# Sliding-window attention into a gated feed-forward: tile 0's values from v as loaded, and 24 unread matrix products ahead of the first turn

## The chip, the cores and the metric

The kernel runs on one core of one Trainium2 chip. The metric is the device time of one execution in microseconds, lower being better. One profiled execution of the kernel gives the trace that is read here. Engines are named as in the profile: PE is TensorE (PEld its weight loads), DVE VectorE, ACT ScalarE, POOL GpSimd, SP SyncE, which only issues transfers.

## The reference

Eight batches of eight heads, 576 positions, head dimension 64. A position sees itself and the 63 before it. The attention output, 4608 rows of 512, goes through h·cos(h) between two matrices.

```python
scores = (1 / sqrt(64)) * q @ k.T                      # q, k, v: (8, 8, 576, 64) f32
rel = pos[:, None] - pos[None, :]
scores = where((rel >= 0) & (rel < 64), scores, -1e9)
attn = exp(scores - max(scores)); attn = attn / sum(attn)
x = (attn @ v).transpose(0, 2, 1, 3).reshape(4608, 512)
h = x @ w_in                                           # (512, 2048)
out = (h * cos(h)) @ w_out                             # (2048, 512) -> (4608, 512) f32
```

## The kernel before

**Tiles and groups.** The 4608 rows are cut into nine tiles of 512 rows (`mt` 0 to 8). A row block has 64 positions, so a batch has nine blocks (`j` 0 to 8), and tile 0 is blocks 0 to 7 of batch 0. Heads go in four pairs (`p`). A block attends to itself and to the block before it: 128 columns of scores for each of the 64 rows of two heads, which makes a unit of 128 x 128. Four units are a group; tile 0 has eight, two for each pair (`g` 0 and 1).

**The steps of a group**, each one or a few instructions: scores on PE (`s`), the row maximum negated on DVE (`m`), four exponentials with their sums on ACT (`e`), the reciprocal of the sums on DVE (`i`), the product of both on POOL or DVE (`n`, tile `w`), four transposes on PE into `tw_ps` (`w`) and a copy to `wT` on DVE or ACT (`c`). When both groups of a pair are there, PE multiplies them with v (`v`, tile `o_ps`) and an engine copies the result to the pair's quarter of `xT` (`x`). Before all that, PE transposes q and k of the pair (`tq`, `tk`) and an engine copies them (`pq`, `pk`). A suffix d, a or p names DVE, ACT or POOL.

**v and its shifted copies.** Block j needs the values of blocks j-1 and j on 128 partitions. The transfers of `load_v` bring blocks 0 and 1 to slot 0 of the tile `v`, 2 and 3 to slot 2, and so on to slot 6, and block 8 to half of slot 7. An odd block finds its two halves in one slot. For an even one the step `z` (`spread_v`) copies halves into the odd slots: block 2 beside block 1 in slot 1, and so on. For batch 0 POOL copies four upper halves (`z.1.p`) and DVE three lower ones (`z.0.d`).

**The feed-forward.** For each of sixteen slices of 128 columns (`ff`) PE adds four products of 128x512, one per pair (`ks`), in `h_ps`; ACT takes the sine, DVE multiplies (`gT`), and PE multiplies by `w_out`. Of tile 0's 64 products some run ahead, as soon as a pair's `xT` is there: `h.0` and `h.1` (three slices each of pairs 0 and 1), `hx.3`, `hx.4` (two products each), and `hl` (pairs 2 and 3 of five slices). The rest follows without a gap in the list.

**What sets the order.** All engines take their instructions strictly in the order in which the program issues them. For tile 0 that order is the string `FIRST`, a list of step names with pair, group and engine; `l` issues the next transfer of a list (`w_in` in three parts, q and k of batch 1, `w_out` in two parts). For all later work, times are given to functions and a loop (`pump`) issues them between the feed-forward's products. In PSUM five named banks and three tiles with the tag "t" are shared by all of these; `H_FIRST` names the banks of `h_ps` in tile 0, `S_FIRST` those of its scores.

Of the kernel before, what the change touches and what calls it, by code (L numbers as in the profile page):

```python
# [10 lines left out]
def _safe_warn(msg, *a, **kw):  # L11
# [3 lines left out]
F32 = mybir.dt.float32  # L15
BF16 = mybir.dt.bfloat16
AF = mybir.ActivationFunctionType
ALU = mybir.AluOpType
# [7 lines left out]
GF = 4  # L26
# [5 lines left out]
PAIRS = 4  # L32
# [3 lines left out]
SKEW = 3  # L36
# [2 lines left out]


FIRST = (
# [6 lines left out]
)  # L48


# [1 line left out]
def kernel(  # L52
# [9 lines left out]
    nc = tc.nc  # L62
    B, H, S, D = q.shape
# [5 lines left out]
    MT = 512  # L69
    TU = MT // 64  # L70
# [4 lines left out]
    att = ctx.enter_context(tc.tile_pool(name="att", bufs=3))  # L75
# [10 lines left out]
    ident = const.tile([128, 128], BF16, name="ident")  # L86
# [5 lines left out]
    st = {}  # L92

    H_FIRST = ("O1", "X0", "X1", "S", "O0") * 3 + ("X0",)
    H_SECOND = ("X0", "X1", "S", "O0", "O1") * 3 + ("t",)
    H_BANKS = ("X0", "O0", "X1", "S", "O1") * 2 + ("X0", "X1", "S", "O0", "O1", "t")
    S_BANKS = ("X1", "S", "X0")
# [3 lines left out]
    def bank(which, name):  # L103
        if which == "t":
            return ps_t.tile([128, 512], F32, tag="t", name=name)
        return ps.tile([128, 512], F32, tag=which, name=name)

    def copy(engine, out, in_):
        {"a": nc.scalar.copy, "p": nc.gpsimd.tensor_copy}.get(engine, nc.vector.tensor_copy)(out, in_)  # L109
# [18 lines left out]
    def halves(tile_):  # L128
        return {name: tile_[:, i * PAIRS * S:i * PAIRS * S + PAIRS * S].rearrange("p (a x) -> p a x", a=PAIRS)
                for i, name in enumerate(("q", "k"))}  # L130

    def rows(b):
        return rowtiles[1 if b == 1 else 0]
# [22 lines left out]
    def values_of(b):  # L156
        return rowtiles[0][:, 0:8 * d_model].rearrange("p (s x) -> p s x", s=8) if b == B - 1 else vtiles[b % 3]

    def load_v(b, c):
        n = 128 if c < 4 else 64  # L160
        vt = values_of(b)[:n, 2 * c if c < 4 else 2 * c - 1]
        nc.gpsimd.dma_start(out=vt.rearrange("p (h d) -> p h d", h=H),  # L162
                            in_=v[b, :, c * 128:c * 128 + n, :].rearrange("h p d -> p h d"))


    def spread_v(b, half, engine="p"):
        vt = values_of(b)
        to, of = ((vt[0:64, 1:7:2], vt[0:64, 2:8:2]), (vt[64:128, 1:8:2], vt[64:128, 0:7:2]))[half]
        if engine == "dma":
            nc.sync.dma_start(out=to, in_=of)  # L170
        else:
            copy(engine, to, of)

    def load_w_in(lo, hi):
        nc.gpsimd.dma_start(out=w_in_sb[:, :, lo:hi], in_=w_in_v[:, :, lo:hi])
# [15 lines left out]
    def put(name, b, p, engine=None):  # L191
        of = st.pop(("t" + name, b, p)).rearrange("d (c p) -> d p c", c=RC)
        to = halves(turned(b))[name][:, p].rearrange("d (p c) -> d p c", c=RC)
        if b or name == "k":
            copy(engine, to, of)
        elif engine == "a":
            nc.scalar.mul(to, of, scale)
        else:
            nc.vector.tensor_scalar(to, of, scale, None, ALU.mult)
# [98 lines left out]
    def g_norm(n, engine="p"):  # L298
        (e, _), rden = st.pop(("e", n)), st.pop(("r", n))
        w = att.tile([128, GF, 128], BF16, tag="w", name="w", bufs=8)  # L300
        u = len(groups[n])
        (nc.gpsimd if engine == "p" else nc.vector).tensor_tensor(out=w[:, 0:u], in0=e[:, 0:u], op=ALU.mult,  # L302
                                in1=rden[:, 0:u].unsqueeze(2).to_broadcast([128, u, 128]))
        st["w", n] = w

    def g_trans(n):
        w, u = st.pop(("w", n)), len(groups[n])
        if n in direct:
            st["tw", n] = t_ps = ps_t.tile([128, GF, 128], BF16, tag="t", name="tw_ps")
            for i in range(u):  # L310
                nc.tensor.transpose(t_ps[:, i], w[:, i], ident)  # L311
            return
        wT = att.tile([128, GF, 128], BF16, tag="wT", name="wT", bufs=20)
        nc.sync.dma_start(out=wT[:, 0:u], in_=w[:, 0:u].rearrange("p u c -> p (u c)"), transpose=True)
        st.update({("wT", unit): wT[:, i] for i, unit in enumerate(groups[n])})

    def g_put(n, engine=None):
        wT, u = att.tile([128, GF, 128], BF16, tag="wT", name="wT", bufs=20), len(groups[n])
        copy(engine, wT[:, 0:u], st.pop(("tw", n))[:, 0:u])
        st.update({("wT", unit): wT[:, i] for i, unit in enumerate(groups[n])})  # L320


    def values(mt, p):
        st["o", mt, p] = o_ps = bank("S", "o_ps") if mt > 1 and p == PAIRS - 1 else ps_t.tile([128, MT], F32, tag="t", name="o_ps")
        for i in range(TU):
            b, j = divmod(mt * TU + i, NU)
            wT = st["wT", (b, p, j)]
            cross = st["cross", (b, p, j)]
            for h in range(2):
                nc.tensor.matmul(out=o_ps[64 * h:64 * h + 64, 64 * i:64 * i + 64],  # L330
                                 lhsT=values_of(b)[:, max(j - 1, 0), 128 * p + 64 * h:128 * p + 64 * h + 64],
                                 rhs=wT[:, 64 * (h ^ cross):64 * (h ^ cross) + 64], start=True, stop=True, skip_group_check=True)


    def put_x(mt, p, engine=None):
        if ("xT", mt) not in st:
            st["xT", mt] = att.tile([128, PAIRS, MT], BF16, tag="xT", name="xT", bufs=2)
        o_ps = st.pop(("o", mt, p))
        copy(engine, st["xT", mt][:, p], o_ps)
# [8 lines left out]
    def first(mt, ff, ks, start, stop):  # L348
        if start:
            st["h", ff] = bank((H_FIRST, H_SECOND, H_BANKS)[min(mt, 2)][ff], "h_ps")  # L350
        nc.tensor.matmul(out=st["h", ff], lhsT=w_in_sb[:, ks, ff * 128:ff * 128 + 128],  # L351
                         rhs=st["xT", mt][:, ks], start=start, stop=stop)

    def skew(mt):
        return 5 if mt < 2 else SKEW

    def last_pairs(mt):
        for ff in range(skew(mt)):
            for ks in range(2, PAIRS):
                first(mt, ff, ks, False, ks == PAIRS - 1)  # L360

    def skewed(mt, ks, n):
        for ff in range(skew(mt) if mt else SKEW):
            first(mt, ff, ks, n == 0, n == PAIRS - 1)

    def last_rows(gT, o_sb):
# [27 lines left out]
    n = n_first  # L394
# [67 lines left out]
    def cast(name, engine):  # L462
        copy(engine, halves(rows(0))[name][:, 0], first_f32[name])
# [10 lines left out]
    def load():  # L474
# [3 lines left out]
    turn_s, turn_h = iter(range(100)), iter(range(100))  # L478
    steps = {"tq": lambda p: transposed("q", 0, (p,)), "tk": lambda p: transposed("k", 0, (p,)),
             "pq": lambda p, engine=None: put("q", 0, p, engine),  # L480
             "pk": lambda p, engine="a": put("k", 0, p, engine),
             "mk": put_masks, "ck": lambda: cast("k", "d"), "l": load, "tb": sine_table, "h": lambda p: skewed(0, p, next(turn_h)), "hl": lambda: last_pairs(0),
             "hx": lambda ff: [first(0, ff, ks, ks == 0, False) for ks in range(2)],
             "z": lambda half, engine=None: spread_v(0, half, engine),
             "s": lambda p, g: g_scores(2 * p + g, next(turn_s) % 5), "m": lambda p, g: g_max(2 * p + g),
             "e": lambda p, g: g_exp(2 * p + g), "i": lambda p, g: g_inv(2 * p + g),
             "n": lambda p, g, engine: g_norm(2 * p + g, engine), "w": lambda p, g: g_trans(2 * p + g),
             "c": lambda p, g, engine=None: g_put(2 * p + g, engine), "v": lambda p: values(0, p),
             "x": lambda p, engine=None: put_x(0, p, engine)}
    for step in FIRST.split():  # L490
        name, *args = step.split(".")
        steps[name](*[int(a) if a.isdigit() else a for a in args])
    load_v(0, 4)
    for c in range(5):
        load_v(1, c)

    for mt in range(n_mt):
# [11 lines left out]
        for ff in range(n_ff):  # L509
# [8 lines left out]
            e = ff % 2  # L518
# [58 lines left out]
```

## Time and profile before

| | us |
|---|---|
| median of 3 runs | 306.96 |
| lowest and highest run | 306.51, 307.69 |
| the profiled execution | 306.41 |
| its span, first to last instruction | 304.4 |
| PE busy in the span | 288.7 (95%) |
| ACT busy | 235.7 (77%) |
| DVE busy | 220.4 (72%) |
| POOL busy | 171.1 (56%) |

All times in the views count from the span's start; 2.0 us of the profiled execution lie around the span. In a row of the timeline stand the start, the duration, the engine, the line, the operation, the tile written and the tile read with their shapes, and how many instructions are merged; in brackets stands idle time just before, with what ended it. Matmuls overlap, so that the start of the next one tells more than the end.

### The profile page before, as it was taken

What the parts mean: (1) busy time and instruction counts of PE and PEld (TensorE: products, weight loads), DVE (VectorE), ACT (ScalarE), POOL (GpSimd) and SP (SyncE); (2) the same over time, 40 slices, a digit from 0 to 9 for tenths busy, and PEclk for the clock granted to TensorE, in tenths of its full rate; (3) what the DMA queues carried; (4) which work ended last, traced back from release to release, by engine and by line L of the source; (5) the groups of instructions that cost most, each with busy time, mean ns of one, the idle gap of its engine ahead of it and who ended that gap; (6) DMA issues with size and microseconds to landing.
All of it is one profiled execution on the core that took longest, in us unless ns stands there. A gap on an engine that the chain in (4) does not pass through costs nothing.

```text
span 304.4 us, 7847 instructions
## 1 busy us (share of the span) xinstructions
PE 288.7 (95%) x2628; PEld 142.1 (47%) x2668; DVE 220.4 (72%) x834; ACT 235.7 (77%) x786; POOL 171.1 (56%) x198
## 2 busy tenths in 40 slices
PE   3769999999999999999999999999999999999996
PEld 3544444544454445444544444444444454454443
DVE  3896889588787878787877787778778877236701
ACT  5997799967997799779987998799869986106600
POOL 8996257977774976497659665967433630000000
PEclk9989999999999999999999999999999999999999
DMA  7999999699969999999999979999994441011012
GB/s 150 181 211 207 207 155 139 105 165 191 225 114 155 225 164 132 154 201 183 138 167 208 189 106 172 157 219 123 180 172 110 87 130 62 0 72 70 0 69 71
DMA packets 165577, 43.88 MB, mean 144 GB/s; under 512 B 154720, under 2 KB 160800, under 8 KB 165536
## 3 DMA queue, kind: packets, MB, share of 16 engines
q0 software_dynamic: 99344, 18.06, 75.1%
q1 hardware_dynamic: 66048, 25.11, 40.2%
q8 instruction: 21, 0.34, 0.5%
q14 instruction: 20, 0.16, 0.2%
q10 hardware_dynamic: 144, 0.20, 0.2%
HBM read 36.70 MB, written 9.44 MB: 152 GB/s over the span
## 4 chain that ended last, share of the span: by engine, by line
PE 88%; DVE 6%; issue 2%; ACT 2%; DMA 1%; POOL 0%; DVEq 0%; POOLq 0%
PE h_ps L351 41%; PE out_ps L534 36%; PE o_ps L330 3%; PE s_ps L261 3%; DVE negm L273 1%; PE out_ps L371 1%; DMA first_f<-in_q_dram 1%; DVE w L302 1%; PE tq_ps L186 1%; DVE s L277 1%; DVE v L109 1%; PE tk_ps L186 1%; PE tw_ps L311 1%; PE s_ps L244 1%; ACT e L288 1%
## 5 line engine op out<-in xcount | busy, mean ns | idle before, releaser
L351 PE MATMUL h_ps<-xT,w_in 128*128 128x512 bf16 x556 | 127.1, 381 | 2.2 <-DVE xT L109 0.6
L534 PE MATMUL out_ps<-w_out,gT 128*128 128x512 bf16 x543 | 123.0, 379 | 1.8 <-issue 1.1
L522 DVE TENSOR_TENSOR gT<-h_ps,sin 128x512 bf16<-128x512 f32 x144 | 95.4, 688 | 33.6 <-ACT sin L519 33.4
L519 ACT ACTIVATE sin<-h_ps 128x512 f32<-128x512 f32 x144 | 82.9, 599 | 34.1 <-PE h_ps L351 32.8
L288 ACT ACTIVATE e<-s,negm 128x128 f32<-128x128 f32 x256 | 98.6, 388 | 0.3 <-DVE negm L277 0.3
L302 POOL TENSOR_TENSOR w<-e,rden 128x512 bf16<-128x512 f32 (+1 forms) x76 | 74.5, 993 | 31.5 <-DVE rden L295 29.1
L351 PEld LDWEIGHTS <-w_in 128*128 128x128 bf16 x576 | 56.0, 98 | 67.1 <-issue 2.7
L534 PEld LDWEIGHTS <-gT 128*128 128x128 bf16 x560 | 53.2, 98 | 62.4 <-issue 0.2
L277 DVE CUSTOM_DVE_ANT_0 s<-s_ps,mask 128x128 f32<-128x128 f32 x256 | 58.0, 284 | 0.1
L288 ACT ACTIVATION_READ_ACCUMULATOR e<-s,negm 128x1 f32 x256 | 48.1, 188 | 0.0
L149 POOL DMA_DIRECT2D rows<-in_q_dram x30 | 25.4, 867 | 25.9 <-DMA T<-rows 16.6
L162 POOL DMA_DIRECT2D v<-in_v_dram x35 | 29.8, 879 | 10.5 <-DMA rows<-in_k_dram 7.3
L109 ACT COPY out_sb<-out_ps 128x512 f32<-128x512 f32 (+1 forms) x18 | 10.1, 563 | 24.2 <-PE out_ps L534 18.7
L295 DVE RECIPROCAL rden<-den 128x4 f32<-128x4 f32 (+1 forms) x80 | 13.8, 172 | 19.2 <-ACT e L288 18.6
L149 POOL DMA_DIRECT2D rows<-in_k_dram x30 | 25.5, 897 | 2.2 <-DMA T<-rows 2.2
L109 DVE CAST xT<-o_ps 128x512 bf16<-128x512 f32 x27 | 17.6, 679 | 6.5 <-PE o_ps L330 6.3
L277 DVE DVE_READ_ACCUMULATOR2_ANT negm<- 128x1 f32 x256 | 21.2, 83 | 0.0
L109 DVE COPY out_sb<-out_ps 128x512 f32<-128x512 f32 x18 | 12.4, 689 | 12.0 <-PE out_ps L534 12.0
L288 ACT ACTIVATE e<-s_ps,negm 128x128 f32<-128x128 f32 x32 | 11.5, 425 | 1.6 <-DVE negm L273 1.6
L261 PE MATMUL s_ps<-T 64*64 64x128 bf16 x512 | 12.1, 221 | 0.0
L261 PEld LDWEIGHTS <-T 64*64 64x64 bf16 x512 | 8.2, 106 | 8.3 <-DVE negm L277 4.4
L330 PEld LDWEIGHTS <-v 128*64 128x64 bf16 x504 | 9.5, 112 | 4.3 <-issue 2.1
(56 smaller groups left out, 146.2 us busy)
## 6 DMA issues: line engine op xcount, KB each, us to landing
out_dram<-out_sb SPq DMA_DIRECT2D x16, 512.0 KB, 6.1
v<-in_v_dram POOLq DMA_DIRECT2D x28, 128.0 KB, 8.3
rows<-in_q_dram POOLq DMA_DIRECT2D x24, 128.0 KB, 5.2
rows<-in_k_dram POOLq DMA_DIRECT2D x24, 128.0 KB, 7.8
w_out<-in_moe_w_out_dram POOLq DMA_DIRECT2D x2, 1024.0 KB, 16.7
w_in<-in_moe_w_in_dram POOLq DMA_DIRECT2D x2, 768.0 KB, 12.4
wT<-w SPq DMA_TRANSPOSE x66, 3.9
out_dram<-out_sb SPq DMA_DIRECT2D x3, 256.0 KB, 2.0
```

The source lines that it names most:

```text
L109: {"a": nc.scalar.copy, "p": nc.gpsimd.tensor_copy}.get(engine, nc.vector.tensor_copy)(out, in_)
L149: nc.gpsimd.dma_start(out=rows(b)[lo:lo + n, slot * 512:slot * 512 + 512].rearrange("p (h d) -> p h d", h=H), in_={"q": q, "k": k}[name][b ...
L162: nc.gpsimd.dma_start(out=vt.rearrange("p (h d) -> p h d", h=H), in_=v[b, :, c * 128:c * 128 + n, :].rearrange("h p d -> p h d"))
L261: nc.tensor.matmul(out=s_ps[cross][to, u].rearrange("p (a t) -> p a t", a=2), lhsT=q_cols(b, p, j)[d], rhs=k_cols(b, p, j)[d], start=True, ...
L277: nc.vector.tensor_tensor_reduce(out=s[:, u], in0=s_ps[:, u], in1=mask[:, 2 - j % 2 if j else 0], scale=-scale if b else -1.0, scalar=BIG, ...
L288: nc.scalar.activation(e[:, u], s[:, u], AF.Exp, bias=negm[:, u:u + 1], scale=1.0 if n < n_first else -1.0, accum_out=den[:, u:u + 1])
L302: (nc.gpsimd if engine == "p" else nc.vector).tensor_tensor(out=w[:, 0:u], in0=e[:, 0:u], op=ALU.mult, in1=rden[:, 0:u].unsqueeze(2).to_br ...
L330: nc.tensor.matmul(out=o_ps[64 * h:64 * h + 64, 64 * i:64 * i + 64], lhsT=values_of(b)[:, max(j - 1, 0), 128 * p + 64 * h:128 * p + 64 * h ...
L351: nc.tensor.matmul(out=st["h", ff], lhsT=w_in_sb[:, ks, ff * 128:ff * 128 + 128], rhs=st["xT", mt][:, ks], start=start, stop=stop)
L519: nc.scalar.activation(sin, h_ps, AF.Sin, bias=math.pi / 2.0)
L522: nc.vector.tensor_tensor(out=gt[:, e], in0=h_ps, in1=sin, op=ALU.mult)
L534: nc.tensor.matmul(out=o_ps[e], lhsT=gT[ff // 2][:, ff % 2, ms * 128:ms * 128 + 128], rhs=w_out_sb[:, ff], start=ff == 0, stop=ff == n_ff - 1)
```

## The change

Tile 0 no longer uses the odd slots of v. `values_first` takes v as it was loaded. An odd block is one product over 128 partitions, as before. An even block is a product over its own 64 rows (the lower half of its slot) and another over the 64 rows of the block before it (the upper half of the slot before). Step `va` issues the first two kinds, step `vb` the products over the block before (`over` in the code). The last pair's are all in `va.3`; there those of the third kind go to a bank of their own (`o2`), and the step `xl` adds them: ACT copies `o2` to SBUF, DVE casts the odd blocks and adds the even ones. Both spreading copies go; block 8, which tile 1 uses, keeps one copy (`spread_last`, on POOL, after tile 0).

The step `warm.24` puts 24 products of the 128 x 128 identity with itself ahead of the first transpose; nothing reads their result.

The list is written in another order. The product of group (1, 0) goes from DVE to POOL, that of group (3, 1) is halved between DVE and POOL (`nh`); `pk.3` and `c.1.0` go from ACT to DVE; `c.3.0` and `x.1` go from DVE to ACT; the transfers of k of batch 1 and of `w_out` are issued behind the last product on POOL. Ahead of `hl` there are now two slices of pairs 0 and 1 and one pair of products (`hx.2`), six products where there were ten; `hl` has three slices instead of five.

On DVE, from the reciprocal of the first group of pair 1 on (`rden` the reciprocals, `negm` the maxima, `w` the product, `v` the spreading copy), before:

```order
L295 RECIPROCAL rden_383<-den_366 128x4
L273 TENSOR_REDUCE negm_385<-s_ps_313 128x4
L302 TENSOR_TENSOR w_396<-e_365,rden_383 128x512
L295 RECIPROCAL rden_404<-den_377 128x4
L273 TENSOR_REDUCE negm_406<-s_ps_348 128x4
L109 COPY wT_434<-tw_ps_324 128x512
L109 COPY wT_438<-tw_ps_399 128x512
L273 TENSOR_REDUCE negm_445<-s_ps_414 128x4
L295 RECIPROCAL rden_447<-den_389 128x4
L109 COPY v0_74<-v0_74 64x3x512
L109 COPY wT_459<-tw_ps_454 128x512
L295 RECIPROCAL rden_478<-den_409 128x4
```

and now:

```order
L300 RECIPROCAL rden_409<-den_390 128x4
L278 TENSOR_REDUCE negm_413<-s_ps_339 128x4
L110 COPY T_178<-tk_ps_354 128x576
L300 RECIPROCAL rden_427<-den_403 128x4
L278 TENSOR_REDUCE negm_431<-s_ps_373 128x4
L110 COPY wT_439<-tw_ps_349 128x512
L300 RECIPROCAL rden_461<-den_417 128x4
L278 TENSOR_REDUCE negm_465<-s_ps_441 128x4
L110 COPY wT_473<-tw_ps_422 128x512
L300 RECIPROCAL rden_497<-den_434 128x4
L278 TENSOR_REDUCE negm_501<-s_ps_451 128x4
L110 COPY wT_514<-tw_ps_475 128x512
```

The product `w` and the copy of `v` are gone from here, the copy of `tk_ps` (`pk.3`) has come, and reciprocals, maxima and copies alternate.

On ACT, from the copy of `tq_ps` of pair 2 to the sine's table, before:

```order
L197 ACTIVATE T<-tq_ps 128x576
L288 ACTIVATE e,den<-s_ps,negm 128x128 x12
L109 COPY T<-tk_ps 128x576
L288 ACTIVATE e,den<-s_ps,negm 128x128 x8
L109 COPY wT<-tw_ps 128x512
L288 ACTIVATE e,den<-s_ps,negm 128x128 x8
L109 COPY wT<-tw_ps 128x512 x2
L346 ACT_TABLE_LOAD
```

and now:

```order
L202 ACTIVATE T<-tq_ps 128x576
L293 ACTIVATE e,den<-s_ps,negm 128x128 x28
L110 COPY wT<-tw_ps 128x512 x2
L110 CAST xT<-o_ps 128x512
L380 COPY over<-o_ps 128x256
L395 ACT_TABLE_LOAD
```

The 28 exponentials behind that copy now stand in one piece; the copies follow them.

On POOL, from the first part of `w_in` on (`rows_73` is q and k of batch 1), before:

```order
L175 DMA w_in<-in_moe_w_in_dram 128x4x512
L175 DMA w_in<-in_moe_w_in_dram 128x4x768
L302 TENSOR_TENSOR w<-e,rden 128x512
L175 DMA w_in<-in_moe_w_in_dram 128x4x768
L142 DMA rows_73<-in_q_dram 128x4x576
L142 DMA rows_73<-in_k_dram 128x4x576
L302 TENSOR_TENSOR w<-e,rden 128x512
L109 COPY v_74<-v_74 64x4x512
L302 TENSOR_TENSOR w<-e,rden 128x512 x3
L178 DMA w_out<-in_moe_w_out_dram 128x8x512
```

and now:

```order
L180 DMA w_in<-in_moe_w_in_dram 128x4x512
L307 TENSOR_TENSOR w<-e,rden 128x512
L180 DMA w_in<-in_moe_w_in_dram 128x4x768 x2
L307 TENSOR_TENSOR w<-e,rden 128x512
L143 DMA rows_73<-in_q_dram 128x4x576
L307 TENSOR_TENSOR w<-e,rden 128x512 x5
L315 TENSOR_TENSOR w<-e,rden 128x256
L143 DMA rows_73<-in_k_dram 128x4x576
L183 DMA w_out<-in_moe_w_out_dram 128x8x512 x2
```

The copy of `v` is gone, and k of batch 1 and the first part of `w_out` now stand behind all products of tile 0; among themselves the transfers keep their order.

The diff, with one line of the list and without the table of step names:

```diff
 FIRST = (
-    "tq.0 mk ck tk.0 pq.0.d pk.0.a s.0.1 tq.1 tk.1 l s.0.0 m.0.1 pq.1.d tq.2 e.0.1 pk.1.d s.1.0 pq.2.a "
+    "warm.24 tq.0 mk ck tk.0 pq.0.d pk.0.a s.0.1 tq.1 tk.1 l s.0.0 m.0.1 pq.1.d tq.2 e.0.1 pk.1.d s.1.0 pq.2.a "
...
-    H_FIRST = ("O1", "X0", "X1", "S", "O0") * 3 + ("X0",)
+    H_FIRST = ("O1", "X0", "O0", "S", "X1") * 2 + ("O1", "X0", "X1", "S", "O0", "X0")
+    O_FIRST = ("X0", "S", "t", "t")
...
+    def spread_last():
+        vt = values_of(0)
+        nc.gpsimd.tensor_copy(vt[64:128, 7], vt[64:128, 6])
...
+    def g_norm_halves(n):
+        (e, _), rden = st.pop(("e", n)), st.pop(("r", n))
+        w = att.tile([128, GF, 128], BF16, tag="w", name="w", bufs=8)
+        for engine, lo, hi in ((nc.vector, 0, 2), (nc.gpsimd, 2, 4)):
+            engine.tensor_tensor(out=w[:, lo:hi], in0=e[:, lo:hi], op=ALU.mult,
+                                 in1=rden[:, lo:hi].unsqueeze(2).to_broadcast([128, hi - lo, 128]))
+        st["w", n] = w
...
+    def warm(n):
+        to = bank("X1", "none_ps")
+        for _ in range(n):
+            nc.tensor.matmul(out=to[:, 0:128], lhsT=ident, rhs=ident, start=True, stop=True)
+
+    def values_first(p, part):
+        if part == "a":
+            st["o", 0, p] = bank(O_FIRST[p], "o_ps")
+        if p == PAIRS - 1:
+            st["o2"] = bank("X1", "o2_ps")[:, 0:MT // 2]
+        lower, upper, both = slice(0, 64), slice(64, 128), slice(0, 128)
+        parts = [(lower, j, j) for j in range(0, TU, 2)] + [(both, j - 1, j) for j in range(1, TU, 2)]
+        over = [(upper, max(j - 2, 0), j) for j in range(0, TU, 2)]
+        if part == "b":
+            parts = over
+        elif p == PAIRS - 1:
+            parts += over
+        for i, (ks, slot, j) in enumerate(parts):
+            apart = p == PAIRS - 1 and ks == upper
+            to = st["o2"][:, 32 * j:32 * j + 64] if apart else st["o", 0, p][:, 64 * j:64 * j + 64]
+            for h in range(2):
+                nc.tensor.matmul(out=to[64 * h:64 * h + 64], lhsT=vt_first(ks, slot, p, h),
+                                 rhs=st["wT", (0, p, j)][ks, 64 * h:64 * h + 64],
+                                 start=part == "a" and i == 0 or apart and j == 0, stop=True, skip_group_check=True)
...
+    def put_x_last():
+        p = PAIRS - 1
+        to, of = (x.rearrange("d (j o c) -> d o j c", o=2, c=64) for x in (st["xT", 0][:, p], st.pop(("o", 0, p))))
+        over = att.tile([128, GF, 128], F32, tag="s", name="over", bufs=4)[:, 0:2].rearrange("d a (j c) -> d (a j) c", c=64)
+        nc.scalar.copy(over, st["o2"].rearrange("d (j c) -> d j c", c=64))
+        nc.vector.tensor_copy(to[:, 1], of[:, 1])
+        nc.vector.tensor_tensor(out=to[:, 0], in0=of[:, 0], in1=over, op=ALU.add)
...
     def skew(mt):
-        return 5 if mt < 2 else SKEW
+        return 5 if mt == 1 else SKEW
...
     def skewed(mt, ks, n):
-        for ff in range(skew(mt) if mt else SKEW):
+        for ff in range(skew(mt) if mt else 2):
             first(mt, ff, ks, n == 0, n == PAIRS - 1)
...
     load_v(0, 4)
+    spread_last()
```

More of the change, by code (lines that the diff above doesn't have):

```diff
@@ L332, in values, with vt_first @@
                                  rhs=wT[:, 64 * (h ^ cross):64 * (h ^ cross) + 64], start=True, stop=True, skip_group_check=True)
+    def warm(n):
[21 more added lines that the diff above has]
+                                 start=part == "a" and i == 0 or apart and j == 0, stop=True, skip_group_check=True)
+    def vt_first(ks, slot, p, h):
+        return values_of(0)[ks, slot, 128 * p + 64 * h:128 * p + 64 * h + 64]
+    def put_x_last():
[5 more added lines that the diff above has]
+        nc.vector.tensor_tensor(out=to[:, 0], in0=of[:, 0], in1=over, op=ALU.add)
     def put_x(mt, p, engine=None):
@@ L481 @@
              "pk": lambda p, engine="a": put("k", 0, p, engine),
-             "mk": put_masks, "ck": lambda: cast("k", "d"), "l": load, "tb": sine_table, "h": lambda p: skewed(0, p, next(turn_h)), "hl": lambda: last_pairs(0),
+             "mk": put_masks, "warm": warm, "ck": lambda: cast("k", "d"), "l": load, "tb": sine_table, "h": lambda p: skewed(0, p, next(turn_h)), "hl": lambda: last_pairs(0),
              "hx": lambda ff: [first(0, ff, ks, ks == 0, False) for ks in range(2)],
-             "z": lambda half, engine=None: spread_v(0, half, engine),
+             "nh": lambda p, g: g_norm_halves(2 * p + g),
              "s": lambda p, g: g_scores(2 * p + g, next(turn_s) % 5), "m": lambda p, g: g_max(2 * p + g),
@@ L487 @@
              "n": lambda p, g, engine: g_norm(2 * p + g, engine), "w": lambda p, g: g_trans(2 * p + g),
-             "c": lambda p, g, engine=None: g_put(2 * p + g, engine), "v": lambda p: values(0, p),
-             "x": lambda p, engine=None: put_x(0, p, engine)}
+             "c": lambda p, g, engine=None: g_put(2 * p + g, engine), "va": lambda p: values_first(p, "a"), "vb": lambda p: values_first(p, "b"),
+             "x": lambda p, engine=None: put_x(0, p, engine), "xl": put_x_last}
     for step in FIRST.split():
```

10 rows, old and new, of the table FIRST are left out of this document.

## The prediction

> **What bounds the kernel now.** I read the page's slices first, to see where PE is not full, then the chain of waits over the first 30 us, then each engine's timeline there.
>
> ```profile
> PE   3769999999999999999999999999999999999996
> ```
>
> A slice is 7.6 us. PE is full from the fourth slice to the last; only the first three, tile 0's attention, have room. What the change can gain lies there; what it loses there comes out at the end, as PE follows without a gap. In the chain of waits (start, duration, what):
>
> ```profile
> 13.47 0.58 DVE negm L273
> 14.04 1.45 DVE w L302
> ...
> 17.50 1.41 DVE v L109
> ...
> 19.37 0.58 DVE negm L273
> 19.94 0.61 DVE xT L109
> ...
> 20.59 0.59 PE h_ps L351
> ```
>
> DVE carries the chain, and 2.86 us of it are the product `w` of group (1, 0) and the copy of `v`, the two that leave DVE. But behind DVE stands ACT with its 32 exponentials. In ACT's timeline:
>
> ```profile
> 9.82 0.65 ACT L197 ACTIVATE T<-tq_ps 128x576 bf16<-128x576 bf16 x1 [0.58 <-PE tq_ps L186]
> 10.36 0.36 ACT L288 ACTIVATE e<-s_ps,negm 128x128 f32<-128x128 f32 x1
> ...
> 14.47 0.71 ACT L109 COPY T<-tk_ps 128x576 bf16<-128x576 bf16 x1
> ...
> 17.73 0.72 ACT L109 COPY wT<-tw_ps 128x512 bf16<-128x512 bf16 x1
> 18.20 0.53 ACT L288 ACTIVATE e<-s_ps,negm 128x128 f32<-128x128 f32 x1
> ...
> 20.04 0.37 ACT L288 ACTIVATE e<-s_ps,negm 128x128 f32<-128x128 f32 x1 [0.18 <-DVE negm L273]
> ...
> 21.33 0.21 ACT L288 ACTIVATION_READ_ACCUMULATOR e<-s_ps,negm 128x1 f32 x1
> ```
>
> Twelve exponentials lie between 10.36 and 14.47, 0.343 each, 1.37 a group. The last group starts at 20.04 and its last sum is there at 21.54. From 10.36 to 20.04 are 9.68 us, six groups are 8.22: 1.46 us are the copies at 14.47 and 17.73, which go to DVE, and the wait for the maximum behind the copy of `v`.
>
> **The start: warm products and the clock.** Twenty-four unread products start when the identity is there (about 1.4 us). The nearest rows are for PE's first transposes and later ones:
>
> ```profile
> 4.43 0.69 PE L186 MATMUL tq_ps<-ident,rows 64*64 64x64 bf16 x18 [4.43 <-ACT rows L109]
> 10.40 0.45 PE L186 MATMUL tk_ps<-ident,rows 64*64 64x64 bf16 x18
> 16.54 0.40 PE L311 MATMUL tw_ps<-ident,w 128*128 128x128 bf16 x4
> ```
>
> The first transposes run at about 0.65 of the later speed. Four products of 128 x 128 take 0.07 each at the later speed (0.40, less one of about 0.19, over three) and by the ratio about 0.11 at the early one: 24 take 2.6 us and end near 4.0, ahead of the transpose at 4.43. They cost nothing unless that is wrong by over 0.4 us. When the clock rose is seen in stretches of equal length (PE busy, the other engines, then the granted clock):
>
> ```profile
> 3.17:6.59 3.42, 2.01 (x43) 1.52 (x45) 2.17 (x7) 2.33 (x5) 3.42 (x7) 1.00 1.08 172
> 6.59:10.00 3.41, 2.89 (x71) 2.44 (x67) 2.75 (x5) 1.69 (x9) 3.41 (x5) 1.00 1.36 176
> ...
> 13.41:16.83 3.42, 2.25 (x34) 1.35 (x34) 3.42 (x8) 3.42 (x20) 3.36 (x3) 1.00 1.23 208
> 16.83:20.24 3.41, 1.68 (x42) 1.22 (x41) 3.41 (x7) 3.23 (x18) 3.33 (x4) 1.00 1.16 211
> 20.24:23.66 3.42, 2.85 (x10) 1.41 (x11) 2.43 (x5) 2.92 (x11) 3.40 (x5) 0.50 1.17 211
> ```
>
> The record of the clock starts at 1.00 and shows its first fall at 20.24, to 0.50 for 3.42 us; the durations say that it was low until about 10. Stretches that were 59% and 49% busy were followed by a low clock, those with 66% and 85% by a full one. With the warm products the first stretch holds 2.01 + 0.8, or 82%, so I take the clock to rise at 6.6. The Trainium skill's page "TensorE: Matmul & The Clock Gate" (Part 1, What's actually happening) has such a window, free-running and 3.4 us long, and lets the clock fall after an idle window; here it fell after one that was half busy, so the measurement decides. By the page's rule alone no low clock could come in the new order either, and the sum below would stand as it is.
>
> What the clock buys is small: the first group's maximum, exponentials and reciprocal are gated by masks and copies, and the next maximum waits for that reciprocal:
>
> ```profile
> 9.27 0.18 DVE L295 RECIPROCAL rden<-den 128x4 f32<-128x4 f32 x1 [0.24 <-ACT e L288]
> 9.37 0.66 DVE L273 TENSOR_REDUCE negm<-s_ps 128x4 f32<-128x512 f32 x1
> ```
>
> It ends at 10.03. The second group's exponentials start at 10.36 only because `pq.2`, late through slow transposes, is in front; with the clock up it fits in ACT's idle 0.58 us, and they start at 10.03. Were the clock up before 4.4, all would come 0.37 earlier.
>
> **ACT after that.** Six groups of 1.37 from 10.03 put the last one at 18.25 and its end at 19.75, against 21.54. The last maximum must be there by 18.25: the reciprocal ahead of it on DVE waits for the last but two (10.03 + 5 x 1.37 + 0.13 = 17.0), then 0.09 and 0.66: 17.75. What ACT sheds falls on DVE, whose queue has lost 2.86 us and got two copies, 0.75 and 0.42 by the first two rows below.
>
> **The tail.** DVE's queue and PE's set it. The durations are from these rows:
>
> ```profile
> 11.22 0.75 DVE L109 COPY T<-tk_ps 128x576 bf16<-128x576 bf16 x1
> ...
> 18.86 0.42 DVE L109 COPY wT<-tw_ps 128x512 bf16<-128x512 bf16 x1
> ...
> 20.54 0.66 DVE L109 CAST xT<-o_ps 128x512 bf16<-128x512 f32 x1
> ...
> 21.79 1.29 DVE L302 TENSOR_TENSOR w<-e,rden 128x512 bf16<-128x512 f32 x1
> ...
> 24.57 1.01 PE L330 MATMUL o_ps<-wT,v 128*64 128x64 bf16 x32
> 25.74 5.32 PE L351 MATMUL h_ps<-xT,w_in 128*128 128x512 bf16 x23 [0.16 <-issue]
> ```
>
> A value product is 0.026 apart ((1.01 - 0.19)/31, about). Halves of 64 rows are in no row; between nothing (two at once) and the same, I take the same, so a pair has 24 instead of 16, +0.2, and tile 0 has 32 more, +0.8, all ahead of the dense part. `x.0` waits for `vb.0`, behind `va.1`, behind `c.1.1`, behind the reciprocal of group (3, 0), which waits for its exponentials (10.03 + 6 x 1.37 + 0.13 = 18.4): `c.1.1` to 18.95, PE to 19.75, `x.0` holds DVE to 20.4. Queued behind it is the last reciprocal, so it loses 0.6. The halved product is at most 0.65 on DVE (half of 1.29): 21.2. PE still does `h.0`, `vb.1` and `va.2` until 21.55, which hides that. Then `w.3.1` to 21.95, its copy to 22.4, `va.3` (24 x 0.026 + 0.17) to 23.2, `vb.2` to 23.4. DVE takes `x.2` first (0.6, to 24.05), then the cast of the odd blocks (half of 0.66) and the addition (0.42, a guess from the same row plus a second operand): `xT` is whole at 24.8.
>
> **The sum.** From 25.74 on PE was dense, with 8 of tile 0's 64 products done: 56 left. In the new order it is dense from 24.83 with 7 done (`h.0`, `h.1`, `hx.2` and one of `hl`): 57 left, at 0.22 each:
>
> ```profile
> 60.84 12.91 PE L351 MATMUL h_ps<-xT,w_in 128*128 128x512 bf16 x58
> ```
>
> Gain: 25.74 - 24.83 - 0.22 = 0.69 us. Nothing in PE's later order changes, so it reaches the end. The profiled execution took 306.41: 305.7. The median of the runs is 306.96, 0.55 above it: 306.3. I take the middle, 306.0.
>
> **POOL and the transfers.** POOL has eight products where it had six and a copy, less half a one:
>
> ```profile
> 8.97 1.55 POOL L175 DMA_DIRECT2D w_in<-in_moe_w_in_dram  x2
> ...
> 13.11 0.76 POOL L142 DMA_DIRECT2D rows<-in_k_dram  x1
> ...
> 17.33 3.22 POOL L302 TENSOR_TENSOR w<-e,rden 128x512 bf16<-128x512 f32 x3
> ...
> 28.08 0.88 POOL L162 DMA_DIRECT2D v<-in_v_dram  x1 [1.38 <-DMA rows<-in_q_dram]
> 30.90 0.69 POOL L162 DMA_DIRECT2D v<-in_v_dram  x1 [1.94 <-DMA rows<-in_k_dram]
> 33.22 0.22 PE L186 MATMUL tk_ps<-ident,rows 64*64 64x64 bf16 x2
> ```
>
> The first product starts one transfer earlier, at 9.8; seven of 1.07 with three transfers of 0.8 between them end at 19.7, when PE turns to their transposes. That costs nothing up to about 1.3 each. k of batch 1 is issued at 21 instead of 13.1, but the queue was delivering q until 28.08 and k until 30.90, in order, and PE asks for k at about 32. Price: nothing. The copy for block 8 (a quarter of 2.25) is needed by tile 1 only.
>
> **Rivals.** (1) A low clock in the tail, chance 0.20. PE's idle places in the new order (12.9 to 13.6, 15.9 to 16.8, 17.9 to 19.0) leave the stretch 13.41 to 16.83 about 61% busy and the next 67%, between what fell and what held. Low from 20.24, PE's tail doubles: `h.0` to `va.2` and `va.3` take 1.2 us more. 306.41 - 0.69 + 1.24 = 307.0, slower than before; on the median 307.5. It decides from about 0.7 us of extra PE time. (2) k of batch 1 late, 0.08: if its 17.5 us from issue to landing were its own and not the queue's, it would land at 38.5, and PE would stand still for 6 us: 312; a gap of 2 us in the queue gives 308. Against it are 28.08 and 30.90. (3) More than the sum, 0.20: the clock is up from the start (0.37), and of PE's idle 0.83 us here
>
> ```profile
> 25.70:41.00 15.30, 14.47 (x213) 6.89 (x216) 12.89 (x20) 10.99 (x20) 3.45 (x5) 1.00 1.39 200
> ```
>
> half goes, since sines start earlier against PE: 306.41 - 0.69 - 0.37 - 0.41 = 304.9. (4) The chain stays, with POOL or DVE in ACT's place, 0.05: 306.4 to 306.9.
>
> **How the numbers follow.** The forecast has 0.47, with its own range 305.4 to 306.6. About 0.5%, 1.5 us, is what a measurement of this kernel can tell from no change, so faster is below 305.4 and slower above 308.5. Faster: 0.16 of rival 3 and 0.06 of the forecast, 0.22. Slower: 0.07 of rival 2 and 0.06 of rivals 1 and 4, 0.13. The same: 0.65. The range takes in most of rivals 1 and 3: 304.7 to 307.6.
>
> **What would show it.** Right: the exponentials in one piece from near 10.0, the last ended near 19.8; `xT` whole near 24.8; PE dense from there; transposes of batch 1 without a wait. Wrong: transposes at 0.69 until 10; a granted clock of 0.50 between 17 and 24; POOL's products above 1.3; the last `xT` after 25.5.

## The result, and the profile after

| | before | after |
|---|---|---|
| median of 20 runs each, same chip | 306.39 | 308.03 |
| lowest and highest run | 305.42, 307.69 | 306.47, 309.97 |
| the profiled execution | 306.41 | 309.07 |
| its span | 304.4 | 307.3 |
| mean granted clock of its span | 0.993 | 0.983 |

The ratio on record is 1.0067 (95% interval 1.0048 to 1.0086), and the medians lie 1.64 us apart, 0.54%: the changed kernel is a little slower. The forecast was 306.0, no change.

Three words are used below. The granted clock is what the profile says PE was allowed, 1.00 being full speed. A low stretch, or a lost one, is 3.41 us at 0.50. PE is dense from the moment at which it runs feed-forward products without a gap; batch 1 starts with the first transposes (`tq_ps`) behind that.

The page's slices of 7.7 us, after (the clock's row under PE's), and last the clock's row before, whose slices are 7.6 us:

```profile
PE   7779999999999999999999999999999999999996
...
PEclk9976999999999999999999999999999999999999
...
PEclk9989999999999999999999999999999999999999
```

PE has more to do in the first three slices, as planned; but the granted clock falls far in the third and fourth, where before it lost one stretch, most of it in the third. The same in stretches (PE busy, its weight loads, DVE, ACT, POOL, then the granted clock):

```profile
12.06:15.47 3.41, 2.39 (x39) 1.52 (x35) 2.73 (x8) 3.41 (x22) 3.39 (x5) 1.00 1.49 199
15.47:18.88 3.41, 1.70 (x36) 1.28 (x33) 2.80 (x9) 3.41 (x22) 3.14 (x4) 1.00 1.17 212
...
18.88:22.29 3.41, 3.41 (x55) 2.26 (x53) 1.36 (x4) 2.12 (x8) 2.29 (x4) 0.50 1.15 211
...
22.29:25.70 3.41, 2.92 (x40) 1.92 (x40) 1.49 (x4) 1.52 (x3) 3.37 (x5) 0.50 1.20 206
...
25.70:29.11 3.41, 3.41 (x9) 1.22 (x8) 1.30 (x3) 1.89 (x5) 3.10 (x4) 0.50 1.21 207
```

Three stretches in a row, 18.88 to 29.1, run at half speed. They follow on one in which PE was busy for half the time (1.70 of 3.41); the one low stretch of the profile before followed on 1.68. In the first low one PE was busy without a gap, and still the next was low. PE's timeline, after:

```profile
1.37 2.74 PE L351 MATMUL none_ps<-ident 128*128 128x128 bf16 x24 [1.37 <-POOL ident masks.py:199]
4.42 0.69 PE L191 MATMUL tq_ps<-ident,rows 64*64 64x64 bf16 x18 [0.30 <-ACT rows L110]
...
5.61 0.38 PE L243 MATMUL s_ps<-mask,ident 128*128 128x512 bf16 x1
...
6.44 0.47 PE L191 MATMUL tq_ps<-ident,rows 64*64 64x64 bf16 x18
...
24.52 0.61 PE L400 MATMUL h_ps<-xT,w_in 128*128 128x512 bf16 x1
25.35 8.07 PE L400 MATMUL h_ps<-xT,w_in 128*128 128x512 bf16 x28 [0.22 <-issue]
33.35 0.48 PE L191 MATMUL tq_ps<-ident,rows 64*64 64x64 bf16 x36
```

The unread products end at 4.1, ahead of the transposes, and the clock is up by about 5.5 (transposes 0.47 at 6.44; before, 0.69 until 10). At the other end the 28 products from 25.35 take 8.07 us, where 23 took 5.32 before, and the first transposes of batch 1 come at 33.35. Before, these stood 2.37 us earlier:

```profile
30.98 0.48 PE L186 MATMUL tq_ps<-ident,rows 64*64 64x64 bf16 x36
```

The span ends 2.9 us later. ACT, DVE and POOL in tile 0:

```profile
9.72 0.37 ACT L293 ACTIVATE e<-s_ps,negm 128x128 f32<-128x128 f32 x1 [0.28 <-DVE negm L278]
...
19.22 0.37 ACT L293 ACTIVATION_READ_ACCUMULATOR e<-s_ps,negm 128x1 f32 x1
```

```profile
20.40 0.17 DVE L300 RECIPROCAL rden<-den 128x4 f32<-128x4 f32 x1
20.60 0.42 DVE L315 TENSOR_TENSOR w<-e,rden 128x256 bf16<-128x256 f32 x1
22.88 0.42 DVE L110 COPY wT<-tw_ps 128x512 bf16<-128x512 bf16 x1 [1.85 <-PE tw_ps L324]
24.64 0.69 DVE L110 CAST xT<-o_ps 128x512 bf16<-128x512 f32 x1 [1.33 <-PE o_ps L369]
...
25.57 0.41 DVE L382 TENSOR_TENSOR xT<-o_ps,over 128x256 bf16<-128x256 f32 x1
```

```profile
20.64 0.85 POOL L315 TENSOR_TENSOR w<-e,rden 128x256 bf16<-128x256 f32 x1 [1.12 <-DVE rden L300]
21.44 0.80 POOL L143 DMA_DIRECT2D rows<-in_k_dram  x1
...
30.36 0.69 POOL L163 DMA_DIRECT2D v<-in_v_dram  x1 [1.56 <-DMA rows<-in_k_dram]
```

The exponentials stand in one piece and end at 19.6. From then on DVE waits for PE, 1.85 and 1.33 us; in the same order at the full clock (`after_filled_small`, below) these two waits are 0.98 and 0.96.

How long a low stretch is: one of 3.41 us at half speed takes 0.0055 off the mean clock of a span of 307, so the mean counts them: none, one, two and three in the rows of this table. All executions by their mean clock (before: of the three series of experiments, taken later, as the clocks of the 20 above are not on record):

| mean clock | after (20) | before (94) |
|---|---|---|
| 0.999 and above | 306.5, 306.7 | 15 runs, 305.0 to 306.9, median 305.3 |
| 0.993, 0.994 | 7 runs, 307.0 to 307.9, median 307.3 | 43 runs, 305.1 to 308.3, median 306.5 |
| 0.987 to 0.989 | 6 runs, 307.7 to 310.0, median 308.7 | 34 runs, 305.4 to 307.5, median 306.3 |
| 0.982, 0.983 | 5 runs, 309.1 to 309.8, median 309.5 | 307.1, 307.1 |

The table shows three things. More than half of the runs after had two or three low stretches, 1.7 on average; but the kernel before had them too, 1.2 on average. After, each one adds about 1 us; before, the first adds about 1.1 and the second nothing. And at the full clock the changed kernel is not faster but slower, by about 1.3 us, though only two of its runs say so.

### The profile page after: what moved, and what is told of

Its sections match the earlier page's. It is cut to its first block, busy times and chain, and to the rows that moved or that the text cites. A ratio compares the mean times of both kernels' runs of the same rounds, so it can differ in the third digit from the quotient of the medians.

```text
span 307.3 us, 7963 instructions
## 1 busy us (share of the span) xinstructions
PE 294.0 (96%) x2685; PEld 146.0 (48%) x2724; DVE 218.7 (71%) x835; ACT 235.3 (77%) x785; POOL 171.2 (56%) x200
## 4 chain that ended last, share of the span: by engine, by line
PE 84%; ACT 7%; DVE 3%; issue 3%; POOL 2%; DMA 1%; POOLq 0%; DVEq 0%; ACTq 0%
PE h_ps L400 41%; PE out_ps L584 34%; ACT e L293 5%; PE s_ps L266 3%; PE o_ps L343 3%; POOL w L307 2%; PE out_ps L420 1%; PE tw_ps L324 1%; PE o_ps L369 1%; DMA wT<-w 1%; DVE gT L572 0%; POOL rows L143 0%; DVE negm L278 0%; ACT T L110 0%; ACT sin L569 0%
## 5 line engine op out<-in xcount | busy, mean ns | idle before, releaser
L307 POOL TENSOR_TENSOR w<-e,rden 128x512 bf16<-128x512 f32 (+1 forms) x77 | 75.4, 991 | 34.7 <-DVE rden L300 29.8
L110 ACT COPY out_sb<-out_ps 128x512 f32<-128x512 f32 (+1 forms) x18 | 10.1, 563 | 24.2 <-PE out_ps L584 18.7
```

## The experiments

Two theories stand against each other. A: the clock falls in tile 0's tail, as the first rival had it. B: the new order itself is slower (the halves, the transfers), whatever the clock. They do not exclude each other. If A, what makes the clock fall: idle time of PE, or how much of PE's array is at work?

**The clock held by unread products** (`after_filled`). Unread products of the identity (fillers) stand where PE waits; `f.8.S` puts eight of them into the bank `S`:

```diff
-    "... e.2.0 w.0.0 ... w.1.0 va.0 ... w.2.0 va.1 ..."
+    "... e.2.0 f.8.S w.0.0 ... w.1.0 f.14.X1 va.0 ... w.2.0 f.6.X1 va.1 ..."
...
+    def fill(n, which):
+        to = bank(which, "none_ps")
+        for _ in range(n):
+            nc.tensor.matmul(out=to[:, 0:128], lhsT=ident, rhs=ident, start=True, stop=True)
```

> The changed kernel with 8, 14 and 6 more unread products of the identity at the three places before the tail of tile 0 where PE stood idle (before w.0.0 0.65 us, before va.0 0.98 us, before va.1 0.46 us). Theory A, the clock: the low clock from 18.9 to 29.1 us comes from these idle places; filled, no stretch of 0.50 comes after 5.2 us, the clock of the run is near 0.999 instead of 0.983 to 0.994, and the median falls from 308.0 to about 306.4 or below. Rival B, the chain: the time is lost to the longer tail itself (24 products a pair, the addition of the last pair), so the clock changes little or the time does not follow it, and the median stays at 307.5 to 308.5. Rival C: the added products delay PE's own work, 308.5 or more.

Measured: 306.32 (306.01 to 307.16, 12 runs), 1.0005 of before (0.9986 to 1.0023); the clock was full in ten runs of twelve and lost one stretch in two. Its stretches about the place that fell:

```profile
13.41:16.83 3.42, 3.42 (x66) 2.39 (x65) 3.25 (x9) 3.42 (x22) 3.40 (x4) 1.00 1.21 209
16.83:20.24 3.41, 2.96 (x67) 2.48 (x64) 2.42 (x8) 3.41 (x21) 3.16 (x4) 1.00 1.16 210
```

PE is busy for 100% and 87% of them. This profile is of one of the two runs that lost a stretch, and lost it earlier, from 7.64 to 11.06, behind a stretch in which PE was busy for 2.20 of 3.42 us (64%). The tail kept its clock.

More work for PE makes the kernel 1.7 us faster by the medians (308.03 to 306.32), or 1.45 when each is taken against the kernel before of its own series (306.39 and 306.13): A holds. But it does not account for all of the 1.64 us, and B is not refuted. The fillers bring the changed kernel level with a kernel before that itself loses a stretch or two in most runs. Full clock against full clock, in the same series, the ten runs here have a median of 306.3 and five of the kernel before 305.2. In the other new orders that kept the clock the same difference is 0.3 (`after_both`) and 0.5 us (`after_filled_small`). So a part of the 1.64 us, somewhere between 0.3 and 1.3, is the order's own; the rest is what the changed kernel loses to the clock beyond what the kernel before loses. This split is an estimate from the table and these medians.

**Without the unread products at the start** (`after_no_warm`: the step `warm.24` taken out).

> The changed kernel without the 24 unread products ahead of the first transpose. Theory A: the first rise of the clock moves back from 5.2 to about 8 to 10 us, e.0.1 starts 0.3 to 0.4 us later and the tail with it; whether and when the clock falls later depends on where its stretches lie, so the median is between 307.5 and 309. Rival: the early products themselves bring the later fall (the clock is raised earlier and falls earlier); then without them the clock reads 0.994 or more and the median falls below 307.3.

Measured: 308.33 (306.61 to 309.91, 8 runs), 1.0059 (1.0030 to 1.0088). That is 0.3 us above the changed kernel by the median and no worse by the ratio (1.0067 there): in time, no effect that can be told. Three of the eight runs lost no stretch, one lost one, three two and one three, so the early products are not what brings the later fall either. Its profiled run kept the full clock in the tail. There the long piece of exponentials starts at 10.79 instead of 9.72, and batch 1 at 31.13.

**The same start for the kernel before** (`before_warm`: 24 of these products ahead of `tq.0`).

> The kernel before with the 24 unread products ahead of its first transpose and nothing else. The chain there is DVE's, gated early by masks and copies: theory A expects 0 to 0.5 us less than before (306.0 to 306.4), and the same single stretch of low clock near 17 to 24 us. If the early products did harm, 306.8 or more.

Measured: 307.01 (305.66 to 310.51, 12 runs), 1.0016 (0.9995 to 1.0037): no gain, where 0 to 0.5 us was expected, and by the median beyond the 306.8 that would have meant harm; the interval takes in no change. One run kept the clock, four lost one stretch, seven two. The profiled one lost two, from 16.2 to 23.0, not the single one that was expected:

```profile
16.40:19.80 3.40, 2.65 (x50) 1.96 (x47) 2.06 (x7) 2.95 (x15) 3.02 (x4) 0.50 1.15 208
19.80:23.20 3.40, 3.16 (x14) 1.52 (x13) 2.70 (x6) 2.77 (x11) 3.38 (x4) 0.53 1.16 210
```

**The clock held in the kernel before** (`before_filled`: `f.14.S` ahead of `w.0.0`, `f.20.X1` ahead of `w.1.1`, `f.6.X1` ahead of `h.0`).

> The kernel before with 14, 20 and 6 unread products at its three idle places of PE (before w.0.0 1.14 us, before w.1.1 1.49 us, before h.0 0.60 us). Theory A: the stretch at 0.50 (20.24 to 23.66 in its trace) goes, its products of h run at 0.22 instead of 0.43 each, and the time falls by 0.8 to 1.2 us to about 305.4. Rival B: PE's clock there is hidden behind DVE's chain, no change within 0.3 us. Rival C: products delay PE's own work, slower.

Measured: 307.24 (306.31 to 309.15, 12 runs), 1.0034 (1.0013 to 1.0054), with the full clock in eleven runs. The clock was held, but theory A's 305.4 was missed by 1.8 us. PE's timeline:

```profile
29.75 0.48 PE L186 MATMUL tq_ps<-ident,rows 64*64 64x64 bf16 x36
...
60.55 0.41 PE L330 MATMUL o_ps<-wT,v 128*64 128x64 bf16 x14 [1.08 <-DMA wT<-w]
...
122.15 0.47 PE L330 MATMUL o_ps<-wT,v 128*64 128x64 bf16 x18 [0.56 <-DMA wT<-w]
```

Batch 1 starts 1.23 us sooner than in the profile before, and the span ends 1.0 later (305.4). PE now waits for transfers of `wT` at 60 and 122 us, where before it had no such wait. Time won in tile 0 is not time won at the end. At the full clock these runs are 2.0 us above the kernel before in the same series (307.2 against 305.2), so fillers can cost later tiles time, and some of the 1.0 us of `after_filled` may be theirs; `after_both`, with its 0.3, has none in the tail.

**Area or busy time, from the products' side** (`after_both`): all 24 products of a pair over 128 rows. It leaves out the selection of rows, so the sums of even blocks take in rows of other blocks; only its time and clock are of use.

```diff
-        lower, upper, both = slice(0, 64), slice(64, 128), slice(0, 128)
+        lower, upper, both = slice(0, 128), slice(0, 128), slice(0, 128)
-            apart = p == PAIRS - 1 and ks == upper
+            apart = p == PAIRS - 1 and i >= TU
```

> The changed kernel with the same 24 products a pair, but all over 128 rows of a slot instead of 16 of them over 64; the sums of even blocks then hold rows that don't belong to them. Time and count of instructions stay the same to the wait. Theory 'area' (the clock goes by how much of PE's array is switched, and products over 64 rows use half): the clock is low in fewer stretches, 306.3 to 307.3. Theory 'busy time' (the clock goes by the share of time that PE has products at all): nothing changes, 307.7 to 308.3.

Measured: 306.62 (306.07 to 307.82, 12 runs), 1.0009 (0.9991 to 1.0028). No run lost more than one stretch: six none, six one; of the changed kernel's twenty, eleven lost two or three. The profiled one lost one, from 18.7 to 22.2 (two answers of the same view):

```profile
15.35:18.76 3.41, 1.75 (x34) 1.30 (x35) 2.74 (x9) 3.41 (x22) 3.22 (x4) 1.00 1.16 210
...
18.70:22.20 3.50, 3.46 (x57) 2.50 (x57) 1.51 (x4) 2.43 (x9) 2.62 (x4) 0.51 1.16 212
```

PE is as busy in it as in the changed kernel's 18.88 to 22.29, but here the next stretch is full. The number of products and the order are the same; only the rows that a product uses differ. So at the same busy time the rows in use decide whether the clock comes back: that rests on two profiled runs and on the counts, none of 12 against 11 of 20. It is not the only thing that keeps the clock low. In `before_warm` the products with v are over 128 rows, PE was busy for 2.65 of 3.40 us of the first low stretch, and the second followed. The fall itself is no different: 1.75 of 3.41 us busy ahead of it.

**Area or busy time, from the fillers' side** (`after_filled_small`: as `after_filled`, each filler over 64 x 64 of the array).

```diff
-            nc.tensor.matmul(out=to[:, 0:128], lhsT=ident, rhs=ident, start=True, stop=True)
+            nc.tensor.matmul(out=to[0:64, 0:128], lhsT=ident[0:64, 0:64], rhs=ident[0:64], start=True, stop=True)
```

> The changed kernel with the same 28 unread products in PE's three idle places as in after_filled, but each over 64 x 64 of the array instead of 128 x 128. They take the same time. Theory 'busy time': as after_filled, 306.3, the clock full. Theory 'area': they count a quarter, the clock falls in the tail as without them, 307.3 to 308.

Measured: 307.27 (305.57 to 310.53, 12 runs), 1.0033 (1.0006 to 1.0060). Seven runs kept the clock, three lost one stretch, two lost three (309.7, 310.5). Between the two theories: with fillers over a quarter of the array the clock was kept more often than without (2 of 20). Whether the whole array keeps it more surely, 7 runs of 12 against 10 of 12 do not tell. Its profiled run kept the clock, and shows the new order without the fall:

```profile
24.81 5.56 PE L405 MATMUL h_ps<-xT,w_in 128*128 128x512 bf16 x25 [0.27 <-DVE xT L382]
30.29 0.48 PE L191 MATMUL tq_ps<-ident,rows 64*64 64x64 bf16 x36
```

**What the halves cost** (`after_16`): 16 products a pair, no second part, no bank of its own and no addition. It leaves out the block before: an even block takes both halves of its own slot, so again only time and clock are of use.

```diff
-        parts = [(lower, j, j) for j in range(0, TU, 2)] + [(both, j - 1, j) for j in range(1, TU, 2)]
-        over = [(upper, max(j - 2, 0), j) for j in range(0, TU, 2)]
+        parts, over = [(both, j - j % 2, j) for j in range(TU)], []
-    "... hx.2 xl tb hl "
+    "... hx.2 x.3.d tb hl "
```

> The changed kernel with 16 products over 128 rows a pair instead of 24, no second part, and no bank of its own nor addition for the last pair (a cast on DVE instead); even blocks then read rows that don't belong to them. It prices the halves: by my sum 32 products of 0.026 us and an addition of 0.42 us that PE waits for, 1.0 to 1.3 us sooner at the first transposes of batch 1 for the same clock. If the tail carries to the end: 1 us under the changed kernel, about 307. If the later stages wait for transfers anyway, the gain at the end is under 0.5 us at the same clock (306.2 instead of 306.5 at the full clock). With 8 products fewer a pair PE has more idle time, so the clock may fall as often.

Measured: 306.26 (305.53 to 308.15, 12 runs), 1.0004 (0.9985 to 1.0023). Eight runs lost one stretch, one lost two, three none (305.8, 306.2, 307.0). PE, and its waits from 36 us on:

```profile
29.51 0.48 PE L191 MATMUL tq_ps<-ident,rows 64*64 64x64 bf16 x36
```

```profile
PE o_ps L343 <- DMA wT<-w: 1.4, 2, 0.9
PE h_ps L397 <- DVE xT L110: 0.9, 1, 0.9
PE o_ps L343 <- DVE v L110: 0.7, 1, 0.7
```

Batch 1's transposes start 1.03 us before those of `after_both`, which lost one stretch in its profile as well: the halves cost what my sum said, 1.0 to 1.3. But the span ends 1.4 later (306.1 against 304.7): 3.0 us of waits have come in later tiles, where `after_both` has 0.8. At the full clock its three runs are level with `after_both` (306.2 and 306.1). So the microsecond does not reach the end, as the second branch of the expectation had it.

**The later stages: transfers or PE** (`before_filled_late`: `before_filled` with `f.18.t` between `hx.4` and `hl`).

> before_filled with 18 more unread products (1.2 us) between the last cast and the remaining products of tile 0, so that the first transposes of batch 1 come at about 30.9, as in the kernel before, at the full clock. Theory 'transfers' (the stages at 60, 74 and 122 us wait for transfers that do not start sooner because PE does): the 1.2 us cost nothing, the wait of 1.1 us on wT at 60 us is gone, 306.1 to 307.2. Theory 'PE carries': 1.2 us later than before_filled, 308.4.

Measured: 307.56 (307.04 to 311.23, 12 runs), 1.0052 (1.0027 to 1.0077): 0.3 above `before_filled`. Batch 1 starts at 30.58, 0.83 us later than there (29.75), so most of the delay cost nothing, as by 'transfers'. Yet in the profiled run the waits did not go:

```profile
62.97 0.41 PE L330 MATMUL o_ps<-wT,v 128*64 128x64 bf16 x14 [2.61 <-DMA wT<-w]
...
125.94 0.47 PE L330 MATMUL o_ps<-wT,v 128*64 128x64 bf16 x18 [0.58 <-DMA wT<-w]
```

Neither theory holds as I put it. But this profile is of the slowest of the twelve runs (311.23), whose clock fell between 64 and 68 us, behind the long wait; the eleven others kept it, and how long their waits were no trace shows.

**Is it POOL's queue?** At 104 to 110 us POOL issues five loads of v, the last of them held up by transfers, and products `w` stand behind. In three kernels those loads were moved behind some products:

```diff
-            at(t0 + (0.5 if b == 2 else 14) + 0.8 * c, load_v, b, c)
+            at(t0 + (0.5 if b == 2 else 17) + 0.8 * c, load_v, b, c)
```

> after_filled with the same later loads of v. Theory 'POOL's loads hold the products back': the wait of 0.39 us on wT at 121.85 us goes, 305.8 to 306.0 where after_filled had 306.3. Theory 'ACT's exponentials set that stage': the wait stays, 306.3.

> after_16 with the same later loads of v. In its profile PE waited 1.4 us on wT at 120 us, 0.7 us on the copy of v and 0.9 us on xT. Theory 'POOL's loads': the 1.4 us go, 305.0 to 305.6, below both kernels; the wait on the copy of v may grow. Theory 'ACT's exponentials': 306.2 as after_16.

> The kernel before, with the loads of v for batches 2 to 7 each 3 steps later in the plan, so that in POOL's queue one product w stands behind the first of five loads and another behind the third, where all products stood behind all five. The kernel before has no wait of PE on wT at 122 us, so by the theory 'POOL's loads hold the products back' it gains nothing, 305.9 to 306.4; it loses up to 1 us if the copies of v on DVE (at 118.7 us) have to wait for the later loads.

Measured: 306.97 (1.0027, 1.0008 to 1.0045), 307.09 (1.0031, 1.0004 to 1.0058) and 306.56 (1.0014, 0.9992 to 1.0037). No gain in any. In `after_filled_late_v` PE still waits there:

```profile
121.56 0.47 PE L343 MATMUL o_ps<-wT,v 128*64 128x64 bf16 x18 [0.52 <-DMA wT<-w]
```

The theory falls. The other theory of these expectations, that ACT's exponentials set that stage, had both kernels unchanged at 306.3 and 306.2; they came out at 307.0 and 307.1, in another series, so it is not borne out either. In the same profile, at the full clock, batch 1 starts at 30.11. But `before_late_v` gave what I should have had first: its tile 0 is that of the kernel before, instruction for instruction, and its profiled run kept the full clock:

```profile
24.51 5.32 PE L351 MATMUL h_ps<-xT,w_in 128*128 128x512 bf16 x23 [0.16 <-issue]
29.75 0.48 PE L186 MATMUL tq_ps<-ident,rows 64*64 64x64 bf16 x36
```

Dense from 24.51, where the profile before had 25.74: the low stretch at 20.24 in that one execution had cost it 1.23 us. `before_filled`, whose fillers held the clock, says the same: batch 1 at 29.75. No version here beats the kernel before.

## Why the prediction was wrong

**The base of the gain: wrong, and of the wrong sign.** The gain of 0.69 us was 25.74 against 24.83. The 25.74 held a low stretch. At the full clock the old order turns dense at 24.51 and reaches batch 1 at 29.75. The new one, with fillers that hold its clock, turns dense at 24.81 and reaches batch 1 at 30.29 (`after_filled_small`; 30.11 in another profile). Like against like, the new order is not shorter but 0.4 to 0.5 us longer, as far as the fillers themselves cost nothing (in `before_filled` they moved the start of batch 1 by nothing). This is the step that failed: the gain is not 0.69 us but a loss of about half a microsecond, before any clock is lost in the new tail. I had quoted the row with 0.50 at 20.24 and not asked what the kernel before would be without it.

**The walk itself: right.** Unread products end at 4.1 (forecast 4.0); clock up by about 5.5 (6.6); exponentials from 9.72 in one piece (10.03), ended 19.6 (19.75); the halved product on DVE 0.42 (at most 0.65), on POOL 0.85; addition 0.41 (0.42); PE dense at the full clock 24.81 (24.83). That is not luck: in `after_filled_small` the steps between agree as well, `w.3.1` done at 21.98 (21.95), `x.2` at 24.09 (24.05), `xT` whole at 24.75 (24.8).

**The clock in the tail: rival 1, with too small a chance and price.** This is the second step that failed: with the clock held in the tail (`after_filled`) the median is 306.3, without it 308.0. I cut the new order into stretches at 13.41 and 16.83, found 61% and 67%, and left it at 0.20. But the stretches begin elsewhere in each execution (the first low one at 20.24 in `before`, 18.88 in `after`, 16.2 in `before_warm`, 7.64 in `after_filled`). In `after` one lay at 15.47 to 18.88, over two of PE's three idle places at once, and was 50% busy, as little as what fell before. The price was put at one stretch, 1.24 us. In the profiled run it was three, and the median run lost two. That PE would then be fully busy, and stay at half speed, was not in the sum: halves over 64 rows take the place of products over 128, and with all products over 128 rows (`after_both`) no run lost a second stretch. In the terms of the sum: `xT` is whole at 25.98 (25.57 + 0.41), not 24.8. PE's last piece begins at 25.35, 0.54 later than at the full clock, with 28 products instead of 25 in it (0.65), and until 29.11 some 8.6 products take 0.22 longer each (1.9): 3.1 in all, against the 3.06 by which 33.35 lies behind 30.29.

The Trainium skill's page "TensorE: Matmul & The Clock Gate" (Part 1, What's actually happening) lets the clock rise after one busy window of about 3.4 us. Here 18.88 to 22.29 was busy throughout and the clock did not rise; with all products over 128 rows, in `after_both`, it did after one such stretch. The measurement decides.

**"Nothing in PE's later order changes, so it reaches the end": wrong.** Kernels whose batch 1 starts between 29.3 and 31.1 end their spans anywhere from 303.8 to 309.2, and not in that order: 29.51 gave 306.1, 29.75 gave 303.8 and 305.4, 30.98 gave 304.4. What is won comes back as waits, above all for `wT` at 60 and 122 us. What the changed kernel loses to the clock does reach the end: by the table, about 1 us for each low stretch.

**Rivals 2 to 4.** k of batch 1, issued at 21.44, was there by 30.36, sooner than before (30.90), and PE did not wait for it: refuted. More gain: the clock was up by about 5.5 and not from the start, and nothing of it reached the end: refuted. As for rival 4, the chain from 9.72 to 17.6 is ACT's exponentials, as in the walk, and neither DVE's nor POOL's products: refuted too.

**Open.** Why the one profile of the kernel before has no wait for `wT` at 122 us, while all others whose trace I read there have one of 0.4 to 1.1, is not settled: POOL's loads of v are not the reason, and PE's lead at the start of batch 1 is not shown to be (`before_filled_late`). Open, too, is how busy a stretch must be for the clock to stay: after 64% it fell (`after_filled`), in the profile before after 66% it held, and the rows in use count as well.

## What to carry to other kernels

Before a gain is taken from one profiled execution, look at the granted clock in the very stretch that the gain is measured in; if that execution was throttled there, the old order must be costed at the full clock first. Cutting matrix products into halves of 64 rows can cost more than their time: here work that kept PE busy, much of it over 64 of the 128 rows, left it at half speed. When fillers make a kernel faster, compare it with the old one at the full clock too, or the clock takes the blame for what the new order costs. And in a kernel with many transfers, a microsecond won early counts only if the later waits have room for it.

## What was unexpected of the hardware

Unread full-array products in PE's idle places made the changed kernel 1.7 us faster (308.03 to 306.32), no faster than the kernel before. PE, busy for the whole of a 3.41-us stretch at half clock, got no higher clock after it when the work was, for the most part, transposes and products over 64 rows. The same program lost none to three such stretches from run to run, worth 306.5 to 310.0 us.
